# Where the weights are clamped: VectorE's step moved to GpSimd, GpSimd's scaling moved to ScalarE

## The chip, the core and the metric

The kernel runs on one core of one Trainium2 chip. A core has five engines that run side by side [...]: TensorE (PE; its weight loads are shown apart as PEld), VectorE (DVE), ScalarE (ACT), GpSimd (POOL) and SyncE (SP), which here only issues transfers. Each engine works through its own queue in order, so an instruction that waits holds up all that stand behind it. The metric is the time of one execution on the device in microseconds, and the median of several executions is compared. The chip's working memory, SBUF, is read by all engines; TensorE writes its results to PSUM, which GpSimd doesn't read in this kernel.

## The reference, cut to what matters

The program is an attention block and then a gated feed-forward block, all in 32-bit floats.

```python
# q, k, v: (batch 8, heads 8, seq 576, head_dim 64); tau = 0.02
scores = scale * q @ k^T
thresh = max(scores) - tau
scores = where(scores >= thresh, scores, -1e9)
attn   = exp(scores - max(scores));  attn /= sum(attn) + 1e-9
x      = attn @ v          # heads side by side: 4608 tokens x 512
g      = x @ w_gate        # 512 x 1536
out    = (g * sigmoid(g) * (x @ w_val)) @ w_out      # 1536 x 512
```

The three weight matrices come into the program as 64-bit floats. The kernel has to turn them into 32-bit floats itself, piece by piece, and that conversion is what the change is about.

## The kernel before, in words

**Attention of the first batch.** A *pair* is two heads of one batch; there are 32 pairs, four to a batch. In the first batch a slot is one tile of up to 128 queries of one pair against all 576 keys. Eight slots (two tiles of each of the four pairs, `early`) come first, then twelve (the three remaining tiles of each pair, `rest`). In a slot (`scores`) TensorE makes the scores (L407, L413); VectorE takes the row maxima (L424); ScalarE makes the threshold (L427) and the exponentials (L428); VectorE masks and sums (L431, with L433 and L434 for the reciprocal `ri`). The tiles of the early slots are normalized by a scaled identity that ScalarE makes (L447). In the twelve later slots (`t >= TA`) the tile itself is scaled by `ri`: the first head's tile by ScalarE (L441), the second head's by GpSimd (L439). The last tile of each pair, 64 queries, holds both heads in one tile and so needs one scaling only. Then `flip` turns the tile on TensorE (L469, L471, and the ends L474, L476, L480), ScalarE copies it out of PSUM (L477, L481, L483), and `attend_tile` multiplies it with v (L500, L503), which ScalarE copies to `xall` (L505). Into the later slots TensorE is also given the first products with the gate and value weights (L517); ScalarE makes the tanh of the gates (L532, L533), VectorE the product (L541), and GpSimd the last factor (L548, `gates`).

**The weights.** They come in 24 pieces of 768 elements a partition. `fetch_weights` has SyncE load the 64-bit words of a piece into one of several places (L280, L277). `split_weights` and `join_weights` then make 32-bit floats:

- ScalarE takes the upper words (L291) and the lower words (L292), the latter into one of three buffers `los`;
- VectorE clamps the upper part between two constants (L298), shifts it left by three bits (L302), and puts the sign back from the upper word (L305);
- GpSimd adds the lower part (L307), after which the piece is a weight and its place is free again.

A piece is split in one slot and joined in the next. There are three exceptions: one slot joins a piece that it has itself split (at about 62 us in the profile), and two slots join two pieces at once (at about 78 and 100 us; `double` in the code), of which the second was split in the same slot. In the double join both clamps come first, then both shifts, then the rest. In the first batch 21 pieces are joined and 22 are split.

**The order of the work.** For the first batch the order on each engine is the order of the lines, written out by hand. For the other seven batches a planner (class `Plan`) sets it: each step is a job with an engine, a cost and the jobs that it depends on, and for each engine the planner takes the job that can start first, by rank. `rest_of_weights` gives the planner what is left of the conversion: the piece that is split but not joined (`lo` is set), and those not yet split (`lo is None`). Its lines are L820 and L823 (ScalarE), L828, L830 and L832 (VectorE) and L834 (GpSimd). The work of a slot there stands in `slot_rest` (maxima L1673 and L1675, exponentials L1698, masks L1700), and GpSimd and ScalarE share the scaling of the tiles (L1723, L1726).

**GpSimd's queue in the first batch** holds the scaling of q (L340), the adds (L307), the scalings of the second head (L439) and the gate products (L548).

Of the kernel before, what the change touches and what calls it, by code (L numbers as in the profile page):

```python
# [13 lines left out]
AF = mybir.ActivationFunctionType  # L14
ALU = mybir.AluOpType
# [12 lines left out]
class Plan:  # L28
# [12 lines left out]
    def job(self, eng, took, fn, *deps, rank=1, lag=0.0, moves=0.0):  # L41
        j = Job(eng, took, fn, rank, lag, moves)
        for d in deps:
            if isinstance(d, Job) and d.end is None:
                d.then.append(j)
                j.waits += 1
            elif d is not None:
                j.ready = max(j.ready, self.after(d, eng) if isinstance(d, Job) else d + self.HOP)
        if not j.waits:
            self.open[eng].append(j)  # L50
        return j
# [61 lines left out]
def kernel(  # L113
# [11 lines left out]
    nc = tc.nc  # L125
# [157 lines left out]
    def words(place, dst, w):  # L283
        return places[place].bitcast(U32).rearrange("p (m n w) -> p m n w", m=dst.shape[1], w=2)[:, :, :, w]

    def split_weights():
        if fetched:
            dst, place = fetched.popleft()
            lo = los[0].rearrange("p (m n) -> p m n", m=dst.shape[1])
            los.rotate(1)  # L290
            nc.scalar.activation(dst, words(place, dst, 1).bitcast(F32), AF.Abs, scale=2.0 ** -96)  # L291
            nc.scalar.activation(lo, words(place, dst, 0), AF.Identity, bias=minus2, scale=-2.0 ** -51)  # L292
            split.append((dst, place, lo))

    def join_weights(n=1):
        steps = [split.popleft() for _ in range(min(n, len(split)))]
        for up, place, lo in steps:
            nc.vector.tensor_scalar(out=up, in0=up, scalar1=1.875 * 2.0 ** -80, scalar2=2.0 ** -111,  # L298
                                    op0=ALU.min, op1=ALU.max)
        for up, place, lo in steps:  # L300
            ub = up.bitcast(U32)
            nc.vector.tensor_scalar(out=ub, in0=ub, scalar1=3, scalar2=None, op0=ALU.logical_shift_left)  # L302
        for up, place, lo in steps:
            ub = up.bitcast(U32)
            nc.vector.scalar_tensor_tensor(out=ub, in0=words(place, up, 1), scalar=0x80000000, in1=ub,  # L305
                                           op0=ALU.bitwise_and, op1=ALU.bitwise_xor)
            nc.gpsimd.tensor_tensor(out=ub, in0=ub, in1=lo.bitcast(U32), op=ALU.add)  # L307
            joined.append(up)
            used.discard(place)
# [82 lines left out]
    def turned(t):  # L392
        return TA <= t < NT
# [4 lines left out]
    def scores(seg, t):  # L398
        qT, kT = seg["qT"], seg["kT"]
        q0 = t * P - seg["q0"]  # L400
        if t < NT:
            pss = [ps_s.tile([P, 2, 512], F32, name="sc") for _ in range(2)]
            for h, hs in enumerate(heads):
                cut_ = D if turned(t) and h == 1 else 0
                for n, lo, to in [(0, 0, D), (0, D, SH), (1, 0, SH)] if cut_ else [(0, 0, SH), (1, 0, SH)]:
                    at_ = (n * SH + lo - cut_) % S
                    nc.tensor.matmul(pss[h][:, n, lo:to], qT[hs, q0:q0 + P], kT[hs, at_:at_ + to - lo],  # L407
                                     start=True, stop=True)
        else:
            pss = [ps_s.tile([P, 2, 512], F32, name="sc")]  # L410
            for n, h in ((0, 0), (1, 1), (1, 0), (0, 1)):
                hs = heads[h]
                nc.tensor.matmul(pss[0][hs, n, 0:SH], qT[hs, q0:q0 + D], kT[hs, n * SH:(n + 1) * SH],  # L413
                                 start=True, stop=True)
        nm, th, ri, tot = statistics("nm", "th", "ri", "tot")
        sm = sums[0]
        sums.rotate(1)
        m = len(pss)
        scs = [ps[:, :, 0:SH] for ps in pss]
        both = pbufs[0].rearrange("p h s -> p (h s)")[:, KM:KM + P]  # L420
        ps = [pbufs[0][:, x, :].rearrange("p (n s) -> p n s", n=2) for x in range(m)]
        pbufs.rotate(1)
        for x in range(m):
            nc.vector.tensor_reduce(out=nm[:, x:x + 1], in_=scs[x], axis=AX.XY, op=ALU.max, negate=True)  # L424
        yield
        for x in range(m):
            nc.scalar.activation(th[:, x:x + 1], nm[:, x:x + 1], AF.Identity, bias=cut, scale=-1.0)  # L427
            nc.scalar.activation(ps[x], scs[x], AF.Exp, bias=nm[:, x:x + 1])  # L428
        yield
        for x in range(m):  # L430
            nc.vector.scalar_tensor_tensor(out=ps[x], in0=scs[x], scalar=th[:, x:x + 1], in1=ps[x],  # L431
                                           op0=ALU.is_ge, op1=ALU.mult, accum_out=sm[:, x, 0:1])
        nc.vector.tensor_reduce(out=tot[:, 0:m], in_=sm[:, 0:m, 0:3:2], axis=AX.X, op=ALU.add)  # L433
        nc.vector.reciprocal(out=ri[:, 0:m], in_=tot[:, 0:m])  # L434
        units = [ident] * m
        if t >= TA:
            for x in range(m):
                if x % 2:
                    nc.gpsimd.tensor_scalar(out=ps[x], in0=ps[x], scalar1=ri[:, x:x + 1], scalar2=None, op0=ALU.mult)  # L439
                else:  # L440
                    nc.scalar.activation(ps[x], ps[x], AF.Copy, scale=ri[:, x:x + 1])  # L441
        yield
        if t < TA:
            units = [dbufs[0][:, x, :] for x in range(m)]
            dbufs.rotate(1)
            for x in range(m):
                nc.scalar.activation(units[x], ident, AF.Copy, scale=ri[:, x:x + 1])  # L447
        unflipped.append((seg, t, both, [(p.rearrange("p n s -> p (n s)"), unit) for p, unit in zip(ps, units)]))
        yield
# [277 lines left out]
    job, pe = plan.job, plan.pe  # L727
# [72 lines left out]
    def rest_of_weights():  # L800

        todo = [(dst, None, place, lo) for dst, place, lo in split] + [(dst, None, place, None) for dst, place in fetched]
        todo += [(dst, srcs, place, None) for dst, srcs, place in wpieces]
        done, joins = {}, []
        for dst, srcs, place, lo in todo:
            m = dst.shape[1]
            j = None
            if srcs:
                def fetch(dst=dst, srcs=srcs, place=place):
                    to = places[place].bitcast(U64).rearrange("p (m n) -> p m n", m=nf)  # L810
                    nc.sync.dma_start(out=to, in_=srcs[0])

                j = job("SP", 0.1, fetch, done.get(place), lag=5.0)
            if lo is None:
                lo = los[0].rearrange("p (m n) -> p m n", m=m)
                los.rotate(1)
                before = joins[-3] if len(joins) > 2 else None

                def up_part(dst=dst, place=place):
                    nc.scalar.activation(dst, words(place, dst, 1).bitcast(F32), AF.Abs, scale=2.0 ** -96)  # L820

                def lo_part(dst=dst, place=place, lo=lo):
                    nc.scalar.activation(lo, words(place, dst, 0), AF.Identity, bias=minus2, scale=-2.0 ** -51)  # L823

                j = job("ACT", 0.93, up_part, j, done.get(place), rank=2)
                j = job("ACT", 1.03, lo_part, j, before, rank=2)
            ub = dst.bitcast(U32)
            j = job("DVE", 0.6, lambda dst=dst: nc.vector.tensor_scalar(  # L828
                out=dst, in0=dst, scalar1=1.875 * 2.0 ** -80, scalar2=2.0 ** -111, op0=ALU.min, op1=ALU.max), j, rank=2)
            j = job("DVE", 0.6, lambda ub=ub: nc.vector.tensor_scalar(  # L830
                out=ub, in0=ub, scalar1=3, scalar2=None, op0=ALU.logical_shift_left), j, rank=2)
            j = job("DVE", 0.96, lambda ub=ub, dst=dst, place=place: nc.vector.scalar_tensor_tensor(  # L832
                out=ub, in0=words(place, dst, 1), scalar=0x80000000, in1=ub, op0=ALU.bitwise_and, op1=ALU.bitwise_xor), j, rank=2)
            j = job("POOL", 1.85, lambda ub=ub, lo=lo: nc.gpsimd.tensor_tensor(out=ub, in0=ub, in1=lo.bitcast(U32), op=ALU.add), j, rank=2)  # L834
            joins.append(j)
            done[place] = j
        return joins
# [1063 lines left out]
    for s, (n, x) in enumerate((n, x) for n in range(len(halved)) for x in range(NU3)):  # L1901
# [29 lines left out]
        if s in WS:  # L1931
            g, place = WS[s]
# [24 lines left out]
    for c in (B - 1, B):  # L1957
# [4 lines left out]
        if c < B:  # L1962
            w = SM // 2
            j = []
# [43 lines left out]
```

## Time and profile before

| | |
|---|---|
| Median of 3 runs | 1380.48 us (1378.73 to 1381.02) |
| Profiled execution, its own time | 1379.44 us |
| Its span, first to last instruction | 1377.3 us |
| Busy: TensorE, VectorE, ScalarE, GpSimd | 1356.8, 1081.5, 875.1, 700.2 us |
| Same from 0 to 160 us | 147.5, 134.9, 124.6, 76.2 us |
| Clamp L298: 21 times, alone / longest | 0.54 / 2.23 us |
| Shift L302: 21 times, alone / beside L439 | 0.56 / 0.98 us |
| Sign L305: 21 times | 0.96 us |
| Add L307 on GpSimd: 21 times | 1.81 us |
| Scaling L439 on GpSimd, 576 elements: 8 times | 1.94 us |
| Scaling L441 on ScalarE, 576 elements: 12 times | 0.79 us |
| Scaling L340 / L1788 of q on GpSimd: 256, 320, 576 elements | 0.92, 1.08, 1.72 us |

In rows of the profile a duration runs from the start to the end of one instruction; on ScalarE and VectorE the next one starts a little before the end of the last, so 12 scalings of 0.79 us follow each other at some 0.67. The brackets at the end of a row say how long the engine sat idle before it, and what ended that.

### The profile page before, as it was taken

The numbers are of one execution on the slowest core, as the hardware profiler recorded it, in microseconds if no ns is written. First come the engines' busy times: TensorE is split into PE (matmuls) and PEld (weight loads), VectorE is DVE, ScalarE is ACT, GpSimd is POOL, SyncE is SP. The second block draws the span as 40 slices with busy tenths as digits, with TensorE's granted clock in tenths as the row PEclk, the third lists the DMA queues.
The fourth block names the chain that finished last, engine by engine and source line by source line (L and its number), as shares of the span: only waits on it lengthen the run. The fifth ranks groups of instructions, "written<-read, shape, count | busy, mean of one in ns | idle before, by whom it ended". The sixth has DMA issues, their size and how long they took to land.

```text
span 1377.3 us, 39288 instructions
## 1 busy us (share of the span) xinstructions
PE 1356.8 (99%) x15630; PEld 1116.4 (81%) x15630; DVE 1081.5 (79%) x2829; ACT 875.1 (64%) x2278; POOL 700.2 (51%) x649
## 2 busy tenths in 40 slices
PE   9988999999999999999999999999999999999998
PEld 6666787778778778887788888878887888999998
DVE  7988988887887777787678877877777776687786
ACT  6888766676755767767766766776677764330330
POOL 2456498844484669533974378436943593000000
PEclk9999999999999999999999999999999999999999
DMA  8734413465513541555155523553065404423421
GB/s 176 208 105 142 99 36 98 122 188 143 174 48 126 143 115 42 170 143 143 32 153 133 146 56 121 139 143 96 27 186 157 112 19 143 158 80 138 154 69 32
DMA packets 208295, 162.33 MB, mean 118 GB/s; under 512 B 166128, under 2 KB 180464, under 8 KB 202736
## 3 DMA queue, kind: packets, MB, share of 16 engines
q1 hardware_dynamic: 203920, 158.86, 40.9%
q8 instruction: 124, 2.03, 0.6%
q10 hardware_dynamic: 4192, 0.95, 0.3%
q14 instruction: 59, 0.48, 0.1%
HBM read 138.28 MB, written 21.50 MB: 116 GB/s over the span
## 4 chain that ended last, share of the span: by engine, by line
PE 91%; DVE 4%; ACT 2%; SPq 1%; DMA 1%; issue 1%; ACTq 0%; DVEq 0%
PE pb L940 18%; PE pa L940 12%; PE px L1420 12%; PE sc L1652 10%; PE xa L1749 9%; PE pe L940 9%; PE po L1216 5%; PE py L1429 5%; PE sc L1101 2%; PE pg L1147 2%; PE pv L1147 2%; PE pv L517 1%; PE pe L1101 1%; SPq L336 1%; PE xa L500 1%
## 5 line engine op out<-in xcount | busy, mean ns | idle before, releaser
L1700 DVE SCALAR_TENSOR_TENSOR pall<-sc,th,pall 128x288 f32<-128x288 f32 x504 | 243.7, 514 | 63.5 <-ACT pall L1698 49.3
L940 PE MATMUL pb<-xall,big 128*128 128x256 f32 x1152 | 273.5, 380 | 0.0
L1698 ACT ACTIVATE pall<-sc,nm 128x288 f32<-128x288 f32 x504 | 231.6, 497 | 34.6 <-DVE pall L1700 34.3
L940 PEld LDWEIGHTS pb<-xall,big 128*128 128x128 f32 x1152 | 216.4, 190 | 31.0 <-issue 2.2
L1728 DVE STREAM_TRANSPOSE pall<-pall 128x576 f32<-128x576 f32 x252 | 190.0, 765 | 59.3 <-ACT pall L1726 42.6
L1726 ACT ACTIVATE pall<-pall,ri 128x288 f32<-128x288 f32 x408 | 186.6, 527 | 25.0 <-DVE ri L1714 24.3
L795 POOL TENSOR_TENSOR hall<-hall,tmp 128x512 f32<-128x512 f32 x80 | 103.6, 1295 | 159.3 <-DVE hall L993 144.0
L940 PE MATMUL pa<-xall,big 128*128 128x256 f32 x768 | 183.3, 382 | 0.0
L940 PEld LDWEIGHTS pa<-xall,big 128*128 128x128 f32 x768 | 143.1, 190 | 22.0 <-issue 2.9
L1652 PE MATMUL sc<-kT,qT 64*32 64x144 f32 (+1 forms) x5376 | 149.8, 345 | 3.4 <-DVE pall L1700 2.2
L1673 DVE TENSOR_REDUCE mx<-sc 128x2 f32<-128x576 f32 x168 | 124.7, 742 | 27.3 <-PE sc L1652 26.9
L1652 PEld LDWEIGHTS sc<-kT,qT 64*32 64x32 f32 x5376 | 97.9, 106 | 57.5 <-issue 21.6
L940 PE MATMUL pe<-xall,big 128*128 128x256 f32 x576 | 137.3, 381 | 0.0
L1749 PE MATMUL xa<-pall,vall 64*32 64x288 f32 x4032 | 132.2, 404 | 1.0 <-DVE hall L993 0.8
L1723 POOL TENSOR_SCALAR pall<-pall,ri 128x288 f32<-128x288 f32 x96 | 95.7, 1010 | 63.6 <-DVE ri L1714 63.5
L940 PEld LDWEIGHTS pe<-xall,big 128*128 128x128 f32 x576 | 108.4, 190 | 17.0 <-issue 2.7
L1749 PEld LDWEIGHTS xa<-pall,vall 64*32 64x32 f32 x4032 | 76.4, 107 | 50.1 <-issue 7.2
L1708 ACT COPY sums<-sums 32x6 f32<-32x6 f32 x336 | 66.6, 198 | 45.1 <-DVE pall L1700 40.5
L1687 ACT COPY mx<-mx 32x6 f32<-32x6 f32 x196 | 38.1, 194 | 60.8 <-DVE mx L1675 58.9
L992 ACT ACTIVATE vall<-tmp 128x512 f32<-128x512 f32 x96 | 60.1, 629 | 23.9 <-POOL tmp L795 9.6
L1429 PE MATMUL py<-wo,hall 128*128 128x256 f32 x336 | 74.8, 379 | 0.0
L1675 DVE TENSOR_REDUCE mx<-sc 128x1 f32<-128x288 f32 x168 | 74.7, 444 | 0.0
(256 smaller groups left out, 2468.2 us busy)
## 6 DMA issues: line engine op xcount, KB each, us to landing
big<-sums_hbm SPq DMA_DIRECT2D x42, 1024.0 KB, 5.3
big<-sums_hbm SPq DMA_DIRECT2D x48, 768.0 KB, 4.8
vall<-in_v_dram SPq DMA_DIRECT2D x112, 144.0 KB, 3.1
out_dram<-big SPq DMA_DIRECT2D x32, 256.0 KB, 3.5
qT<-in_q_dram SPq DMA_DIRECT2D x112, 72.0 KB, 4.8
kT<-in_k_dram SPq DMA_DIRECT2D x112, 72.0 KB, 3.1
wo<-in_moe_w_gate_dram SPq DMA_DIRECT2D x16, 384.0 KB, 3.8
wo<-in_moe_w_val_dram SPq DMA_DIRECT2D x16, 384.0 KB, 4.5
```

The costliest lines, as they stand in the source:

```text
L795: return lambda: nc.gpsimd.tensor_tensor(out=out, in0=a, in1=b, op=op)
L940: nc.tensor.matmul(ps[:, i], w[:, k_, i * P:(i + 1) * P], x[:, k_, :], start=first and i == k_ == 0, stop=True, skip_group_check=True)
L1420: nc.tensor.matmul(ps, a[:, f, :], ws[n][:, f, :], start=bank_ not in begun, stop=True, skip_group_check=True)
L1429: nc.tensor.matmul(ps(), a[:, f, i * P:(i + 1) * P], operands[o][:, f, :], start=first and f == 0, stop=True, skip_group_check=True)
L1652: nc.tensor.matmul(pss[h][(slice(g * G, (g + 1) * G), *part)], qT[hs, col:col + G], kT[hs, c * SH + keys[0]:c * SH + keys[1]], start=True, ...
L1673: rs.append(job("DVE", 0.72, lambda n=n, tile_=tile_: nc.vector.tensor_reduce(out=mx[:, n:n + 2, 0], in_=tile_[:, :, 0:SH], axis=AX.X, op= ...
L1698: ej = job("ACT", 0.42, lambda x=x, n=n: nc.scalar.activation(ps[x], scs[x], AF.Exp, bias=nm[:, n:n + 1]), ej, *((masks[h, 0], masks[h, 1] ...
L1700: masks[x] = job("DVE", 0.45, lambda x=x, n=n: nc.vector.scalar_tensor_tensor(out=ps[x], in0=scs[x], scalar=th[:, n:n + 1], in1=ps[x], op0 ...
L1723: scaled.append(job("POOL", 1.02, lambda x=x, n=n: nc.gpsimd.tensor_scalar(out=x, in0=x, scalar1=ri[:, n:n + 1], scalar2=None, op0=ALU.mul ...
L1726: scaled.append(job("ACT", 0.46, lambda x=x, n=n: nc.scalar.activation(x, x, AF.Copy, scale=ri[:, n:n + 1]), rj, rank=rank))
L1728: seg["turned"].append(job("DVE", 0.72, lambda both=both: nc.vector.transpose(out=both, in_=both), *scaled, rank=rank))
L1749: nc.tensor.matmul(holds[a].ap()[x * G:(x + 1) * G, 0:SH].rearrange("d (i q) -> d i q", q=G), vr[rs, h, j, ds], p[rs, h, :, j, :], start=( ...
```

## The change

The clamp leaves `join_weights` and goes to the end of `split_weights`, on GpSimd, in place and with the same two constants. In the later slots of the first batch ScalarE scales the tiles of both heads, so L439 is gone. In `rest_of_weights` a piece that was split in the first batch has been clamped there, so its clamp L828 on VectorE is left out; the pieces not yet split keep theirs.

```diff
@@ split_weights
             nc.scalar.activation(dst, words(place, dst, 1).bitcast(F32), AF.Abs, scale=2.0 ** -96)
             nc.scalar.activation(lo, words(place, dst, 0), AF.Identity, bias=minus2, scale=-2.0 ** -51)
+            nc.gpsimd.tensor_scalar(out=dst, in0=dst, scalar1=1.875 * 2.0 ** -80, scalar2=2.0 ** -111, op0=ALU.min, op1=ALU.max)
             split.append((dst, place, lo))
@@ join_weights
         steps = [split.popleft() for _ in range(min(n, len(split)))]
-        for up, place, lo in steps:
-            nc.vector.tensor_scalar(out=up, in0=up, scalar1=1.875 * 2.0 ** -80, scalar2=2.0 ** -111,
-                                    op0=ALU.min, op1=ALU.max)
         for up, place, lo in steps:
             ub = up.bitcast(U32)
             nc.vector.tensor_scalar(out=ub, in0=ub, scalar1=3, scalar2=None, op0=ALU.logical_shift_left)
@@ scores
         if t >= TA:
             for x in range(m):
-                if x % 2:
-                    nc.gpsimd.tensor_scalar(out=ps[x], in0=ps[x], scalar1=ri[:, x:x + 1], scalar2=None, op0=ALU.mult)
-                else:
-                    nc.scalar.activation(ps[x], ps[x], AF.Copy, scale=ri[:, x:x + 1])
+                nc.scalar.activation(ps[x], ps[x], AF.Copy, scale=ri[:, x:x + 1])
@@ rest_of_weights
+            inside = lo is not None
             if lo is None:
                 ...
             ub = dst.bitcast(U32)
-            j = job("DVE", 0.6, lambda dst=dst: nc.vector.tensor_scalar(
+            j = j if inside else job("DVE", 0.6, lambda dst=dst: nc.vector.tensor_scalar(
                 out=dst, in0=dst, scalar1=1.875 * 2.0 ** -80, scalar2=2.0 ** -111, op0=ALU.min, op1=ALU.max), j, rank=2)
```

The order of instructions that follows: on GpSimd a piece's clamp stands ahead of the add of the piece before it. From piece 0 on the queue reads clamp 1, add 0, clamp 2, add 1 and so on, with the q scalings and gate products between; around the exceptions it reads clamp 7, add 6, add 7, clamp 8, clamp 9, add 8, a q scaling, clamp 10, add 9, add 10, clamp 11, gate product, clamp 12, add 11, and likewise clamp 14, add 13, add 14, clamp 15, gate product, clamp 16, add 15. TensorE's order and SyncE's are unchanged. In the planner's part the missing job moves some instructions of VectorE, ScalarE and GpSimd by a few places, within about the first ten slots after the first batch.

## The prediction

> **What bounds the kernel now.** I read the page first: engine shares, then the waits of TensorE, then TensorE, VectorE and GpSimd over the first batch in order of time. Sections 1 and 5 of the page and the windows (columns: length, then busy time of PE, PEld, DVE, ACT and POOL with instruction counts, granted clock, DMA share, GB/s):
>
> ```profile
> PE 1356.8 (99%) x15630; PEld 1116.4 (81%) x15630; DVE 1081.5 (79%) x2829; ACT 875.1 (64%) x2278; POOL 700.2 (51%) x649
> 40.00:60.00 20.00, 18.91 (x157) 14.22 (x157) 18.21 (x41) 19.18 (x43) 8.61 (x6) 1.00 0.90 216
> 60.00:80.00 20.00, 17.72 (x138) 13.19 (x139) 17.16 (x30) 16.85 (x30) 10.90 (x6) 1.00 0.40 121
> 100.00:120.00 20.00, 17.00 (x136) 12.71 (x134) 17.55 (x34) 15.80 (x33) 12.97 (x7) 1.00 0.55 197
> ```
>
> TensorE is busy all but 1377.3 - 1356.8 = 20.5 us. Of these, 160 - 147.5 = 12.5 us lie in the first 160 us, the stretch that the change edits. So a gain ends near 12 us; a loss has no such end. The waits of TensorE from 20 to 150 us (total, times, longest):
>
> ```profile
> PE pv L517 <- ACT big L477: 6.4, 4, 2.3
> PE sc L407 <- DVE pall L431: 2.9, 4, 1.0
> ```
>
> The timeline puts its pauses at 28.59 (0.41), 41.66 (0.81), 69.73 (2.28), 84.54 (1.04), 91.58 (1.70), 105.97 (0.65), 109.69 (0.71), 113.40 (1.64), 132.15 (0.80) and 161.77 (1.58). Most have one root. The copies L477 stand in ScalarE's queue behind the exponentials L428, which wait for the row maxima L424, which stand in VectorE's queue behind the weight join L298, L302, L305. VectorE, late with a join, is what ends last here. The timeline shows why it is late:
>
> ```profile
> 62.53 1.83 POOL L307 TENSOR_TENSOR big<-big,extra 128x768 uint32<-128x768 uint32 x1 [0.57 <-ACT big L291]
> 62.55 2.23 DVE L298 TENSOR_SCALAR big<-big 128x768 f32<-128x768 f32 x1 [0.16 <-ACT big L291]
> 70.62 1.87 POOL L439 TENSOR_SCALAR pall<-pall,ri 128x576 f32<-128x576 f32 x1 [2.31 <-DVE ri L434]
> 70.94 0.98 DVE L302 TENSOR_SCALAR big<-big 128x768 uint32<-128x768 uint32 x1
> 84.91 1.27 POOL L548 TENSOR_TENSOR hall<-hall,tmp 128x512 f32<-128x512 f32 x1
> 85.52 1.08 DVE L298 TENSOR_SCALAR big<-big 128x768 f32<-128x768 f32 x1
> ```
>
> A VectorE tensor-scalar takes 0.54 alone. Behind a GpSimd tensor-tensor it waits until that ends (2.23, 1.08); beside a GpSimd tensor-scalar it takes 0.98.
>
> [...] L832[...] took 1.98 at 152.63 behind an add that began at 151.97, against 0.96 alone. [...] 288 elements take 1.00 (L1723), 576 take 1.72 (L1788), so 2.5 ns an element.
>
> **The change, part by part.** Numbering the pieces 0 to 21 in order of their splits:
>
> - Removed: L298 on VectorE, 21 times, 14.6 us in all with its collisions; one L828 of 0.55 in the slots after. L439 on GpSimd, 8 x 1.94 = 15.5 us, and with it its collisions with L302 (0.98 instead of 0.56, so 0.42 a time).
> - Added to GpSimd: 22 clamps. No two-operation tensor-scalar is in the trace. By the line through L1723 and L1788 it is 1.72 + 192 x 0.0025 = 2.2 us. [...] From above: a second operation as dear as the first, 0.28 + 768 x 0.005 = 4.1. I take 2.3, since L439 beside VectorE took 0.22 more than L1788 of its shape[...].
> - Added to ScalarE: 8 scalings L441 at 0.67 from start to start, 5.4 us. Where ScalarE next waits for maxima (2.28 before 82.61, 1.50 before 89.31) that costs nothing; where it runs without a gap, as from 67.5 to 80.3 and 89.3 to 102.1, all behind it is 0.67 later, the next L291 included.
> - The wait moves. L302 now waits for the clamp, a stage longer: ScalarE's L291, then GpSimd. And the GpSimd queue is in order: a new piece's clamp stands ahead of the old piece's add, which stands ahead of gate products and q scalings. No DMA is issued by a moved step; SP refills a place after L305, so its transfers follow VectorE.
>
> Usually a piece is clamped one slot before its L302, and the clamp is hidden. Five times it is not: piece 7 (split and joined in one slot), 10 and 14 (a double join whose second piece was split in that slot), and 11 and 15 (their clamps stand behind the two late adds of the double join). Walking the queues with trace durations and 2.2 us a clamp gives these leads of the changed kernel (plus is ahead):
>
> 1. To 41.7 us. Three L298 go (0.54 + 0.76 + 0.54 = 1.84); two q scalings now overlap L302 and give back some 0.6: +1.2. To 59 us TensorE's slot falls from 5.73 to about 5.57 (scores 1.28 rather than 1.44) three times: **+1.7**.
> 2. Piece 7. L291 ends at 62.5 - 1.7 = 60.8, clamp to 63.1. GpSimd's add of piece 6 is next and ready[...]. L302 and L305 to 66.4, the transpose L705 0.4, maxima at 66.75 against 66.71: **0**.
> 3. Piece 10. L291 comes 0.67 later (L441), ends 77.55; clamp to 79.8; L302 to 80.4, two L305 to 82.3, L705; maxima at 82.7 against 81.86: **-0.85**.
> 4. Piece 11. Add 9 from 81.45 takes 2.39 as at 80.79, add 10 to 85.65, clamp to 87.85[...]; L302 and L305 to 90.5; maxima at 90.45 against 88.53: **-1.9**.
> 5. Pieces 14 and 15, the same again: maxima at 105.95 against 103.25 and 114.15 against 110.36: **-2.7**, then **-3.8**.
> 6. 114 to 142 us: single joins, clamps hidden. VectorE is 0.54 to 0.96 shorter a slot, ScalarE 0.67 longer in some; TensorE's pause at 132.15 (0.80) fills: **-3.0**.
> 7. From 142 us the masks wait for ScalarE, which waits for TensorE's transposes, so the missing L828 (0.55) is slack. After 160 us TensorE is busy within 8 us of the rest and the lead is carried to the end.
>
> At 2.3 a clamp, five deciding pieces add 5 x 0.1: **-3.5 us**. The profiled execution took 1379.44 (span 1377.3 and 2.1 around it): 1382.9. It lies 1.0 under the median shown, 1380.48, so the median becomes **1384.0**.
>
> **Rivals.** (a) *The clamp is cheap; faster.* All in walk items 2 to 5 hangs on its price, about 5 us of total per 1 us of clamp. The lead is zero at 2.2 - 3.0 / 5 = 1.6 us[...]. [...] Against it: 2.5 ns an element for every one-input row. (b) *The clamp is dear; GpSimd becomes the bound.* At 2.9 the five pieces add 3.0 more, 1387; at 4.1 four clamps, four adds and a gate in each 21.8 us (16.4 + 7.3 + 1.3 = 25) no longer fit: 3 us in each of two such rounds on top of 5 x 1.8, about 1399. For it: two operations instead of one. Against: one-input rows are already above the cost of two-input ones per element (1.72 for 576, 1.81 for 768), so both operations may be in the price. (c) [...] the blocks of 1.8, 1.15 and 1.15 fall away, -3.5 becomes +0.5: no change, 1380. Against it: at 62.53 GpSimd won by 0.02 us, and its next instruction needs no semaphore from another engine. (d) *Everything is in slack:* 1380 too; the pauses listed speak against it.
>
> **How the numbers follow.** Forecast 0.47 (its own range 1381.5 to 1387), (b) 0.21, (c) and (d) together 0.18, (a) 0.14. A measurement of this kernel can tell about 0.2%, 2.8 us, from no change, and the forecast lies just past that: two thirds of it, 0.31, count as slower and 0.16 as the same. Slower 0.31 + 0.21 = 0.52; faster 0.13 of (a) and 0.02 of (c) = 0.15; the same 0.16 + 0.16 + 0.01 = 0.33. The range, 1377.5 to 1391, leaves out about half of (a) and the dearer half of (b).
>
> **What would show it.** Right: no clamp row on VectorE, a GpSimd clamp row of 22 at 2.2 to 2.5; L302's waits on GpSimd in a few large pieces (7, 10, 11, 14, 15) rather than spread; TensorE ahead at 59 us and behind at 115; pauses before L517 near 91 and 113 longer; no change of busy time after 200 us. Wrong: a clamp under 1.6 us or over 2.9, L302 starting at the very end of a clamp with a tensor-tensor queued behind it, or a moved order of the planned slots after 140 us that makes TensorE wait there, which I cost at nothing because TensorE has 7 us of its own work (two groups of L1147) in each such slot.

## The result, and the profile after

The changed kernel takes 1383.65 us in the median of 10 runs (1381.25 to 1384.9), the kernel before 1380.05 us (10 runs beside it, 1378.06 to 1381.35). The ratio is 1.0026, with a 95% interval from 1.0016 to 1.0036: 3.6 us slower, where 3.5 were forecast. The number came out by luck: the clamp costs less than half of what was assumed, the first batch loses next to nothing, and most of the 3.6 us lies after 150 us, in a step that the forecast had costed at nothing.

The profiled execution took 1384.36 us, with a span of 1382.3 us. Its engine shares, and its windows for the same three stretches as before (length, then busy time of PE, PEld, DVE, ACT and POOL, granted clock, DMA share, GB/s):

```profile
PE 1360.3 (98%) x15630; PEld 1118.5 (81%) x15630; DVE 1069.2 (77%) x2807; ACT 879.2 (64%) x2286; POOL 708.6 (51%) x663
40.00:60.00 20.00, 19.52 (x169) 14.89 (x170) 16.68 (x37) 17.82 (x41) 12.01 (x9) 1.00 0.91 222
60.00:80.00 20.00, 17.50 (x120) 12.71 (x119) 13.43 (x24) 17.72 (x30) 11.16 (x9) 0.91 0.36 120
100.00:120.00 20.00, 16.95 (x140) 12.46 (x139) 15.84 (x28) 17.30 (x35) 12.76 (x9) 1.00 0.56 197
```

VectorE has 12.3 us less work and TensorE 3.5 us more, for the same 15630 matmuls: the clock column points to why, since it shows 0.91 from 60 to 80 us where the kernel before had 1.00. From 40 to 60 us TensorE is busier than before (19.52 against 18.91 us): there the change wins, as foretold.

The waits of TensorE from 20 to 150 us, which answer to those of before (6.4 us for L477, 2.9 us for L431):

```profile
PE pv L512 <- ACT big L472: 6.6, 4, 2.5
PE tp L464 <- ACT tmp L528: 1.2, 2, 0.6
PE tp L464 <- ACT pall L436: 0.6, 1, 0.6
...
PE sc L405 <- DVE pall L429: 0.2, 1, 0.2
```

The wait for VectorE's masks fell from 2.9 to 0.2 us. The wait for ScalarE's copies did not fall, and its longest is now 2.5 us. A new one stands beside it: the transposes wait for ScalarE's gate copies (L528), 0.6 us a time, because ScalarE now has the second scaling ahead of these. (The kernel with the scalings alone, below, has the same waits.)

The clamps on GpSimd in the first 145 us, by shape (busy time and mean in ns, then idle time before them):

```profile
L293 POOL TENSOR_SCALAR big<-big 128x768 f32<-128x768 f32 x16 | 16.8, 1047 | 33.9 <-ACT big L291 33.9
L293 POOL TENSOR_SCALAR wo<-wo 128x768 f32<-128x768 f32 x6 | 7.4, 1238 | 13.3 <-ACT wo L291 13.3
```

A clamp takes 1.1 us in the mean, not 2.3. The timeline at 61 and 85 us:

```profile
60.72 0.83 POOL L293 TENSOR_SCALAR big<-big 128x768 f32<-128x768 f32 x1 [3.40 <-ACT big L291]
61.51 1.81 POOL L305 TENSOR_TENSOR big<-big,extra 128x768 uint32<-128x768 uint32 x1
61.58 2.17 DVE L300 TENSOR_SCALAR big<-big 128x768 uint32<-128x768 uint32 x1 [2.10 <-POOL big L293]
84.69 1.27 POOL L543 TENSOR_TENSOR hall<-hall,tmp 128x512 f32<-128x512 f32 x1
84.75 1.63 DVE L300 TENSOR_SCALAR big<-big 128x768 uint32<-128x768 uint32 x1 [0.18 <-POOL big L293]
86.41 1.46 DVE L303 SCALAR_TENSOR_TENSOR big<-wo,big 128x768 uint32<-128x768 uint32 x1
```

Alone a clamp takes 0.83 us. What was foretold for a shift behind a clamp holds to 0.2 us: right behind the clamp GpSimd starts its add (L305) or gate product (L543), and the shift, 0.06 or 0.07 us later, lasts until 0.4 us after that has ended. It takes 2.17 and 1.63 instead of 0.56 us, 1.6 and 1.1 us more, where 1.8 and 1.15 were foretold. This comes on top of the wait for the clamp, which the brackets give apart (2.10 and 0.18 us).

Where the time is lost is seen when TensorE's pauses after 150 us are read in order of time (start, length, engine, line, and in brackets the idle time before it and what ended that). The kernel before has one of over 0.25 us in this stretch, until 289 us:

```profile
161.77 2.13 PE L1652 MATMUL sc<-kT,qT 64*32 64x288 f32 x64 [1.58 <-DVE pall L1700]
```

The changed kernel has three, and the first is followed by scores at a low clock (0.50 from 164 to 166 us; 3.57 instead of 2.13 us for the same 64 matmuls):

```profile
163.50 3.57 PE L1648 MATMUL sc<-kT,qT 64*32 64x288 f32 x64 [2.45 <-DVE pall L1696]
183.61 4.68 PE L1745 MATMUL xa<-pall,vall 64*32 64x288 f32 x140 [0.66 <-ACT mx L1683]
229.45 2.13 PE L1648 MATMUL sc<-kT,qT 64*32 64x288 f32 x64 [1.22 <-DVE pall L1696]
```

(2.45 - 1.58) + 0.66 + 1.22 = 2.75 us are new pauses, and 3.57 - 2.13 = 1.44 us clock.

VectorE's queue ahead of these masks tells what is late. Before:

```profile
156.59 0.76 DVE L1790 STREAM_TRANSPOSE kT<-kT 128x576 f32<-128x576 f32 x1
157.55 0.17 DVE L1691 TENSOR_REDUCE nm<-mx 128x6 f32<-128x12 f32 x1 [0.19 <-ACT mx L1687]
157.63 0.77 DVE L1728 STREAM_TRANSPOSE pall<-pall 128x576 f32<-128x576 f32 x1
158.47 0.52 DVE L1700 SCALAR_TENSOR_TENSOR pall<-sc,th,pall 128x288 f32<-128x288 f32 x1
```

And after:

```profile
157.98 1.41 DVE L1724 STREAM_TRANSPOSE pall<-pall 128x576 f32<-128x576 f32 x2
159.32 0.12 DVE L1687 TENSOR_REDUCE nm<-mx 128x6 f32<-128x12 f32 x1
159.37 0.76 DVE L1789 STREAM_TRANSPOSE qT<-qT 128x576 f32<-128x576 f32 x1
160.20 0.52 DVE L1696 SCALAR_TENSOR_TENSOR pall<-sc,th,pall 128x288 f32<-128x288 f32 x1
```

With one job of 0.6 us less in its books the planner has put two transposes of `pall` ahead of these masks, where there was one, and also the transpose of `qT`, which came behind them before (at 163.25 us). TensorE waits for the masks. They start at 160.20 instead of 158.47 us; of these 1.7 us TensorE was 0.9 late already at 137 us.

### The profile page after: what moved, and what is told of

Same layout as the page of the kernel before. It is cut to its first block, busy times and chain, and to the rows that moved or that the text cites. A ratio compares the mean times of both kernels' runs of the same rounds, so it can differ in the third digit from the quotient of the medians.

```text
span 1382.3 us, 39260 instructions
## 1 busy us (share of the span) xinstructions
PE 1360.3 (98%) x15630; PEld 1118.5 (81%) x15630; DVE 1069.2 (77%) x2807; ACT 879.2 (64%) x2286; POOL 708.6 (51%) x663
## 4 chain that ended last, share of the span: by engine, by line
PE 92%; DVE 4%; ACT 2%; issue 1%; POOL 1%; DMA 1%; SPq 0%; DVEq 0%; ACTq 0%; POOLq 0%
PE pb L936 18%; PE pa L936 12%; PE px L1416 12%; PE sc L1648 10%; PE xa L1745 9%; PE pe L936 9%; PE po L1212 5%; PE py L1425 5%; PE sc L1097 2%; PE pg L1143 2%; PE pe L1097 1%; PE sc L405 1%; PE pv L1143 1%; PE pv L512 1%; PE tp L466 1%; PE xa L495 1%
```

## The experiments

The theories. *The forecast's*: the first batch loses, because the clamp makes joins late; the missing planner's clamp is slack. *The planner's*: the moved order of the planned slots costs the 3.6 us. A third is about TensorE's *clock*: that it falls behind pauses such as those of 2.50 and 2.11 us in the changed kernel's profile (to 0.71 from 66 to 71 us, to 0.70 from 90 to 95), and that this is part of the loss. All runs stand beside runs of the kernel before on the same chip; its median was 1380.18 us in the first four, 1379.93 in the next four, 1379.66 in the next three and 1380.32 in the last.

### The planner's clamp put back

```diff
-            j = j if inside else job("DVE", 0.6, lambda dst=dst: nc.vector.tensor_scalar(
+            j = job("DVE", 0.6, lambda dst=dst: nc.vector.tensor_scalar(
```

> The changed kernel with one part undone: the planner's clamp of the piece split in the first batch stays on VectorE, although GpSimd has clamped it (clamping twice changes nothing), so the planned slots have the order of before. Forecast as recorded (waits for the clamp in the first batch; the missing planner job is slack): no change from the changed kernel, 1383.5. Theory from the two traces (TensorE is 0.87 behind at 151 us, 1.73 at 163.5, 4.8 at 229, so over half is lost in planned slots whose order moved): some 2.5 us faster than the changed kernel, near 1381; lead of TensorE at 140 us unchanged, the pause at 163.5 back to about 1.6, that at 229 gone.

Measured: 1380.02 us, ratio 1.0001 (0.9993 to 1.0009). All that differs from the changed kernel is one VectorE instruction more, and the order that the planner then chooses; the 3.6 us are gone. Its windows from 160 to 260 us:

```profile
160.00:180.00 20.00, 18.36 (x196) 14.72 (x195) 18.39 (x49) 15.46 (x41) 11.12 (x11) 1.00 0.28 62
180.00:220.00 40.00, 39.70 (x652) 32.01 (x651) 33.84 (x101) 27.87 (x81) 39.56 (x37) 1.00 0.19 39
220.00:260.00 40.00, 39.89 (x494) 31.55 (x500) 35.94 (x110) 27.02 (x77) 34.56 (x37) 1.00 0.43 131
```

The changed kernel has 17.55, 39.23 and 38.78 us there.

### The planner's part alone

The kernel before, with GpSimd's clamp for the last piece of the first batch only, and with the planner as in the changed kernel:

```diff
-            j = job("DVE", 0.6, lambda dst=dst: nc.vector.tensor_scalar(
+            j = j if inside else job("DVE", 0.6, lambda dst=dst: nc.vector.tensor_scalar(
```

> The kernel before in the whole first batch, its clamps on VectorE and its scaling shared as it was, except that the last piece of the weights, the one that the planner joins in the second batch, is clamped on GpSimd and the planner's clamp of it (0.55 us of VectorE) is left out, so that the planned slots stand in the order of the changed kernel. The forecast's theory (the loss lies in the first batch and the missing planner's clamp is slack): 1380.2 us, ratio within 0.9990 to 1.0010, and TensorE waits for L1696 as before (1.6 us). The planner theory (the moved order of the planned slots costs the whole 3.6 us): 1383 to 1384.5 us, ratio 1.002 to 1.003, with TensorE's wait for the masks at 160 us near 2.4 us and busy shares of 180 to 260 us as in the changed kernel (39.2 and 38.8 of 40 us).

Measured: 1383.36 us, ratio 1.0027 (1.0016 to 1.0037). TensorE's pauses, which are those of the changed kernel though the first batch is that of before:

```profile
164.40 2.13 PE L1657 MATMUL sc<-kT,qT 64*32 64x288 f32 x64 [2.64 <-DVE pall L1705]
183.04 4.68 PE L1754 MATMUL xa<-pall,vall 64*32 64x288 f32 x140 [0.65 <-ACT mx L1692]
228.88 2.13 PE L1657 MATMUL sc<-kT,qT 64*32 64x288 f32 x64 [1.22 <-DVE pall L1705]
```

The forecast's theory falls. This part alone costs 3.4 us, (2.64 - 1.58) + 0.65 + 1.22 = 2.9 us of it in pauses. Here the clock stayed up after the first pause (1.00 from 160 to 180 us). In this profile it fell once, to 0.91 in the window from 60 to 80 us, behind a pause of 2.27 us before 69.73 us that the kernel before has too (2.28 us, with the clock at 1.00); from there TensorE became 1.6 us late (93.16 instead of 91.58 us at the next value product), and that has nothing to do with the planner.

### The order without the instruction

```diff
-            j = j if inside else job("DVE", 0.6, lambda dst=dst: nc.vector.tensor_scalar(
+            j = job("DVE", 0.6, lambda dst=dst, inside=inside: inside or nc.vector.tensor_scalar(
```

> The changed kernel, with the planner's clamp kept as a job of 0.6 us that issues no instruction: the planned slots stand in the order of the kernel before, and VectorE has still 0.55 us less work. It tells the order from the missing instruction. Order theory: 1380 us, ratio 0.999 to 1.001, 180 to 260 us busy as before (39.7 to 39.9 of 40 us each). Missing instruction theory (something that VectorE now does sooner collides): 1383.6 us, ratio 1.002 to 1.003. The forecast's theory (first batch): 1383.6 us too, but the run with the planner's clamp put back already speaks against it.

Measured: 1381.17 us, ratio 1.0009 (1.0001 to 1.0017). The profile has the pause of before at the masks (1.57 us), none at 183 and 229 us, and busy times of 39.71 and 39.89 us from 180 to 260 us. So it is the order, not the missing 0.55 us, that makes the pauses. The median is 1.1 us over that of the run with the clamp in place; the intervals overlap, and whether anything stands behind it was not settled. In the two profiles it doesn't come from the planned slots: TensorE is 1.1 us behind at 41 us already (41.30 against 40.16 us) and 1.0 at the masks (163.71 against 162.75 us).

### The clamps alone, and the scalings alone

Both are the kernel before with one part of the change, and with the planner as before. The clamps alone:

```diff
             nc.scalar.activation(lo, words(place, dst, 0), AF.Identity, bias=minus2, scale=-2.0 ** -51)
+            nc.gpsimd.tensor_scalar(out=dst, in0=dst, scalar1=1.875 * 2.0 ** -80, scalar2=2.0 ** -111, op0=ALU.min, op1=ALU.max)
...
-            nc.vector.tensor_scalar(out=up, in0=up, scalar1=1.875 * 2.0 ** -80, scalar2=2.0 ** -111,
-                                    op0=ALU.min, op1=ALU.max)
```

> The kernel before with only the clamps of the first batch moved to GpSimd; second-head scaling stays on GpSimd, planner's clamp stays. Forecast as recorded with the clamp at 2.3 us: slower than before by 2 to 4. Theory from the traces (a clamp takes 0.83 alone, 1.05 to 1.4 beside VectorE): the 1.85 us won by 59 us stay to a good part, 0 to 1.5 us faster than before, 1378.5 to 1380.

The scalings alone:

```diff
-                if x % 2:
-                    nc.gpsimd.tensor_scalar(out=ps[x], in0=ps[x], scalar1=ri[:, x:x + 1], scalar2=None, op0=ALU.mult)
-                else:
-                    nc.scalar.activation(ps[x], ps[x], AF.Copy, scale=ri[:, x:x + 1])
+                nc.scalar.activation(ps[x], ps[x], AF.Copy, scale=ri[:, x:x + 1])
```

> The kernel before with only the scaling moved to ScalarE; clamps stay on VectorE, planner unchanged. Forecast as recorded has 0.67 us of lateness in the slots where ScalarE has no gap, and 0.42 us saved on each of 8 shifts: within 1 us of before. Theory from the traces: the two pauses of 0.6 at the transposes appear, and before the L517 of those slots nothing is won: 1 to 1.5 us slower than before, 1381.4.

Measured: clamps alone 1379.62 us, ratio 0.9994 (0.9986 to 1.0002); scalings alone 1381.31 us, ratio 1.0008 (1.0000 to 1.0016). Neither differs from before by as much as the planner's part. With the clamps alone TensorE has two new pauses, in which GpSimd's scaling comes late behind a clamp and a gate product:

```profile
87.98 0.66 PE L467 MATMUL tp<-pall 128*128 128x128 f32 x4 [2.41 <-POOL pall L437]
110.86 1.11 PE L467 MATMUL tp<-pall 128*128 128x128 f32 x4 [2.04 <-POOL pall L437]
```

### The change with the scaling back on GpSimd

```diff
-                nc.scalar.activation(ps[x], ps[x], AF.Copy, scale=ri[:, x:x + 1])
+                if x % 2:
+                    nc.gpsimd.tensor_scalar(out=ps[x], in0=ps[x], scalar1=ri[:, x:x + 1], scalar2=None, op0=ALU.mult)
+                else:
+                    nc.scalar.activation(ps[x], ps[x], AF.Copy, scale=ri[:, x:x + 1])
```

> The changed kernel with the other part undone: the second head's tiles of the later slots are scaled by GpSimd again; clamps stay on GpSimd, the planner's part as changed. Forecast as recorded: GpSimd has 8 x 1.94 us more before its clamps and adds, so the clamps of pieces 7, 10, 11, 14 and 15 come later still: slower than the changed kernel by 2 or more, 1386. Theory from the traces (ScalarE's 8 extra scalings make the pauses before the transposes at 118 and 137, 0.6 each, and hold the maxima's exponentials): faster than the changed kernel by 1 to 2 us in the first batch, 1382; the loss after 150 us stays.

Measured: 1382.63 us, ratio 1.0017 (1.0009 to 1.0025), 1 us under the changed kernel, with 4.4 us of waits for the planned masks (4.3 in the changed kernel, 2.2 before) and 4.8 us for GpSimd's scalings. The planner's part costs here too: it is all that tells this kernel from the one with the clamps alone, which took 3 us less. Both have a mean clock of 0.9969, so these 3 us are not the clock.

### Every clamp twice

In the changed kernel, after GpSimd's clamp:

```diff
+            nc.gpsimd.tensor_scalar(out=dst, in0=dst, scalar1=1.875 * 2.0 ** -80, scalar2=2.0 ** -111, op0=ALU.min, op1=ALU.max)
```

> The changed kernel with every clamp of the first batch done twice on GpSimd (22 more instructions, the second does nothing new): GpSimd has 22 x 0.83 to 1.4 us more work and each join comes later by one clamp. The forecast's sum (a clamp at 2.3 us, joins late by it reach the maxima and TensorE nearly in full): 5 us more per us of clamp, so with 0.9 us more 1388 us, ratio 1.005 to 1.007. Trace theory (VectorE waited only three times, 2.9 us in all, for a clamp, and most joins have slack): 1383.5 to 1385.5, ratio 1.0025 to 1.004.

Measured: 1389.71 us, ratio 1.0069 (1.0053 to 1.0085), 6.1 us over the changed kernel. The second clamp took 0.92 us in the mean. The pauses before the value product in this run, at places where the changed kernel has 2.50 and 1.69 us:

```profile
69.48 2.93 PE L513 MATMUL pv<-xall,big 128*128 128x256 f32 x6 [3.43 <-ACT big L473]
...
118.39 1.57 PE L513 MATMUL pv<-xall,big 128*128 128x256 f32 x6 [2.52 <-ACT big L473]
```

The pause between them is shorter than in the changed kernel (1.69 instead of 2.11 us). VectorE's waits for the clamps (total, times, longest), in the changed kernel and in this one:

```profile
DVE big L300 <- POOL big L293: 2.9, 3, 2.1
DVE big L301 <- POOL big L294: 6.2, 4, 2.9
```

TensorE reaches the third value product at 118.39 instead of 113.55 us, 4.8 us later. Here the forecast's theory holds: its slope, 5 us of time for 1 us of clamp, gives 4.6 for 0.92 us, and 6.1 was measured. The trace theory, with slack behind most joins, falls. A part of the 6.1 us may be clock: the mean clock was 0.9952 against 0.9975, which by the slope in the last section goes with 2 us.

### Filling the pauses

In the changed kernel, and in the one with the planner's clamp back, ahead of the four value products, 5, 4, 3 and 0 times:

```diff
+            nc.tensor.matmul(ends[0][:, P:P + TC], ones[:, 0:P], ones, start=True, stop=True)
```

> The changed kernel with 12 dummy matmuls into unused columns of a bank (5, 4, 3 and 0 of them ahead of the four value products of the first batch, some 0.43 us each), so that TensorE is not idle where it waits for the copies L472 [...]. Clock theory (the pauses over 2 us halve the clock for some 3 us, which cost 1.4 us at 68 us and 1.0 us at 92 us): clock 1.00 in 60:100, TensorE up to 2 us sooner at 142 us, time 1381.5 to 1383. If what is won there is lost again at the masks at 160 us, or if the dummies delay the products by themselves: 1383 to 1385, ratio 1.002 to 1.003.

> The changed kernel with the planner's clamp put back and the same 12 dummy matmuls. Clock theory: 1377.5 to 1379.5 us, ratio 0.998 to 0.9995, faster than both kernels. If the first batch's lead is given back later: 1380 us, ratio 0.9995 to 1.0005.

Measured: 1387.49 us, ratio 1.0055 (1.0043 to 1.0067), and 1383.91 us, ratio 1.0035 (1.0023 to 1.0047). The dummies filled nothing. They waited themselves, for ScalarE's copy out of the bank that they wrote to, up to 3.2 us. A second attempt wrote into the bank of the value product:

```diff
+            nc.tensor.matmul(ps[:, 0], ones[:, 0:P], ones, start=True, stop=True)
```

> The changed kernel with 12 dummy matmuls as before (5, 4, 3 and 0), but into the bank of the value product itself, ahead of the matmuls that overwrite it, so that they wait for no copy of ScalarE; TensorE's pauses of 2.5, 2.1 and 1.7 us ahead of L512 are filled with 2.2, 1.7 and 1.3 us of work. Clock theory (pauses over 2 us halve the granted clock for some 3 us, 1.4 us lost at 68 us and 1.0 us at 92 us): clock 1.00 in 60:100, TensorE 1.5 to 2.5 us sooner at 142 us; with the masks at 160 us unchanged the time is 1381.5 to 1383. If what is won there is lost again at 160 us: 1383.6, ratio 1.002 to 1.003. If the dummies wait too or come late: over 1384.

> The same dummies in the changed kernel with the planner's clamp put back. Clock theory: 1377.5 to 1379.3 us, ratio 0.998 to 0.9995, faster than both kernels. If the lead won in the first batch is given back later: 1380 us, ratio 0.9995 to 1.0005.

Measured: 1386.03 us, ratio 1.0039 (1.0026 to 1.0052), and 1382.37 us, ratio 1.0017 (1.0011 to 1.0024). They waited again, as the changed kernel's row shows when filled (its first ten matmuls are the five dummies, two each):

```profile
68.40 2.43 PE L512 MATMUL pv<-pall 128*128 128x256 f32 x10 [2.51 <-ACT big L473]
```

The other two groups of dummies waited 2.12 and 1.74 us. A dummy reads nothing that ScalarE writes there, so these waits before the value product are for the PSUM bank, which the copies of the transposed tiles have to empty first, and not for data; the wait's name doesn't tell the two apart. What a fallen clock costs these runs don't tell, since no pause was filled. They price delay: from the first of the dummies to the row behind them five take 2.26 us (68.40 to 70.66) and four 1.83 (91.68 to 93.51), so one more is 0.43 us, and 12 are 5.2 us of TensorE's time. The first attempt made both kernels nearly 4 us slower, the second 2.4 us.

### Two scalings on ScalarE, six on GpSimd

The kernel with the clamps alone, and:

```diff
+    scaled_by = deque([1, 1, 0, 1, 0, 1, 1, 1])
...
-                if x % 2:
+                if x % 2 and scaled_by.popleft():
                     nc.gpsimd.tensor_scalar(out=ps[x], in0=ps[x], scalar1=ri[:, x:x + 1], scalar2=None, op0=ALU.mult)
```

> The kernel before, with the clamps of the first batch on GpSimd, the planner as before, and only two of the eight second-head scalings on ScalarE: the third and the fifth, those for which TensorE waited 2.41 us (at 87.98) and 2.04 us (at 110.86) in the run with the clamps alone. The other six stay on GpSimd. If these two waits are the whole loss there: 1375.5 us, ratio 0.9965. Theory of the shifted pause: GpSimd's late scaling only covers a pause that VectorE's maxima make anyway; the two waits go, and TensorE stands ahead of the value product instead, for the bank that ScalarE's copies empty after the maxima: some 2 us at 89 us and 1.5 us at 112 us, so that only 0.5 us a time are won: 1378.5 to 1379.5 us, ratio 0.9985 to 0.9995.

Measured: 1377.82 us, ratio 0.9985 (0.9978 to 0.9992). It is faster than the kernel before and the changed one, 2.5 us under the runs of before beside it. The pauses lie where the theory of the shifted pause put them:

```profile
66.96 1.56 PE L517 MATMUL pv<-xall,big 128*128 128x256 f32 x6 [1.23 <-ACT big L477]
...
89.05 1.56 PE L517 MATMUL pv<-xall,big 128*128 128x256 f32 x6 [2.12 <-ACT big L477]
...
110.37 1.56 PE L517 MATMUL pv<-xall,big 128*128 128x256 f32 x6 [1.78 <-ACT big L477]
...
158.83 2.13 PE L1653 MATMUL sc<-kT,qT 64*32 64x288 f32 x64 [1.60 <-DVE pall L1701]
```

The waits of 2.41 and 2.04 us for GpSimd are gone and 2.12 and 1.78 us for the bank have come. Behind them is VectorE, as before: the maxima of that tile start at 86.01 us here and at 86.26 us with the clamps alone. After each of these three pauses TensorE starts 2.5 to 3.0 us sooner than in the kernel before (66.96 against 69.73, 89.05 against 91.58, 110.37 against 113.40), and at the masks it is 2.9 us ahead. Beside their own runs of before, this kernel is 1.9 us faster than the clamps alone. That may be the clock and nothing else: the mean clock was 0.9994 against 0.9969, and by the slope in the last section that goes with 2.2 us.

## Why the prediction came out right, by wrong steps

The time at which TensorE reaches the same work, in the profiles of five kernels (us; the first four columns are the rows L500 and three times L517 of the kernel before):

| | v product | value 1 | value 2 | value 3 | masks | last mask pause |
|---|---|---|---|---|---|---|
| before | 59.92 | 69.73 | 91.58 | 113.40 | 161.77 | 289.44 |
| changed | 58.07 | 68.10 | 90.84 | 113.55 | 163.50 | 294.22 |
| planner's clamp back | 58.08 | 68.14 | 90.89 | 113.60 | 162.75 | 290.42 |
| planner's part alone | 59.93 | 69.73 | 93.16 | 114.98 | 164.40 | 293.67 |
| two scalings | 58.20 | 66.96 | 89.05 | 110.37 | 158.83 | 286.49 |

**Step 1, to 59 us, +1.7: right.** Measured 59.92 - 58.07 = +1.85.

**The price of the clamp, 2.3 us: wrong by a factor of two and more.** It takes 0.83 us alone and 1.1 in the mean. This was the condition that the prediction named for its own failure (under 1.6 us), and rival (a) is the one that had the clamp cheap. The 768 elements in 0.83 us are 1.1 ns an element, against a slope of 2.5 ns in the rows of scaling (1.00 us for 288 elements, 1.72 for 576). Those multiply by an operand that holds one number per partition; the clamp has two constants. They were the nearest rows, but not the same operation. Which of the differences makes the price was not tested.

**Steps 2 to 5, leads of 0, -0.85, -1.9, -2.7 and -3.8 at pieces 7, 10, 11, 14 and 15: wrong in size, right in kind.** The order of the queues and the five pieces came as described. So did the shift that lasts until GpSimd's next instruction has ended (2.17 us behind the clamp of piece 7, 1.63 at 84.75 us), and so rival (c), without these blocks, falls. But each of these clamps is 1.4 us shorter than the 2.2 of the walk: the maxima start at 65.08, 80.83, 87.80, 103.11 and 110.50 us, which is +1.63, +1.03, +0.73, +0.14 and -0.14. Doubling the clamp bore out the slope of these steps upwards (4.6 foretold, 6.1 measured); the value put into it was wrong.

**Step 6, -3.0 at 142 us: wrong in size.** At 132 us the lead is 132.15 - 132.39 = -0.24. The pause filled there from 0.80 to 0.31 us, as said; the added scaling on ScalarE, which the step let pass at these slots, makes two pauses of 0.6 us ahead of the transposes, and the lead is -0.9 when the planned slots begin.

**Step 7, the planned slots, 0: this is the step that failed.** It reasoned that a missing VectorE step is slack where TensorE has work. It didn't ask what the planner does when one of its jobs is gone. From value 3 to the last mask pause the kernel before takes 289.44 - 113.40 = 176.0 us, the planner's part alone 178.7, the changed kernel 180.7 and the changed kernel with the planner's clamp back 176.8. The prediction had named such a moved order as what would make it wrong, and had dismissed it because of 7 us of TensorE's own work in each slot; the pauses of 2.45, 0.66 and 1.22 us show that this doesn't cover it.

**How the sum still came out: by two errors of opposite sign, which is luck.** The clamps of the five deciding pieces (at 60.72, 76.94, 83.90, 99.65 and 106.60 us) took 0.82 or 0.83 us. With 0.83 the prediction's own slope gives 3.5 - 5 x (2.3 - 0.83) = -3.9 us, a gain. The planner's part adds 3.4 measured: -0.5. Some 4 us are left to the measured 3.6, and they belong to the first batch: the change without the planner's part came out 0.2 us faster than the runs beside it, not 3.9.

Where that gain went is shown in part. One place is GpSimd's queue. With the clamps alone its scaling stands between the clamp of piece 7 and the add:

```profile
61.07 0.83 POOL L293 TENSOR_SCALAR big<-big 128x768 f32<-128x768 f32 x1 [3.41 <-ACT big L291]
61.88 2.12 POOL L437 TENSOR_SCALAR pall<-pall,ri 128x576 f32<-128x576 f32 x1
61.93 0.56 DVE L300 TENSOR_SCALAR big<-big 128x768 uint32<-128x768 uint32 x1 [2.11 <-POOL big L293]
63.97 1.82 POOL L305 TENSOR_TENSOR big<-big,extra 128x768 uint32<-128x768 uint32 x1
```

VectorE's shift takes 0.56 us there; the maxima start at 64.18 us, and the first value product at 67.19 us after a pause of 1.25 us. With the planner's clamp put back, which differs only in the scalings, the add stands right behind the clamp and the shift takes 2.17 us; the maxima start at 65.11 us, the product at 68.14 us after 2.52 us. So moving the scaling away let the add forward, and the add holds VectorE up.

Another place is the clock: behind the pauses at the first two value products it is 0.71 from 66 to 71 us and 0.70 from 90 to 95 in the changed kernel, and 1.00 in the kernel before. TensorE's order is the same in both kernels, so the same rows can be compared, first changed, then before:

```profile
68.10 2.93 PE L512 MATMUL pv<-xall,big 128*128 128x256 f32 x6 [2.50 <-ACT big L472]
72.33 1.09 PE L495 MATMUL xa<-big,vall 128*64 128x128 f32 x16
69.73 1.56 PE L517 MATMUL pv<-xall,big 128*128 128x256 f32 x6 [2.28 <-ACT big L477]
72.34 1.09 PE L500 MATMUL xa<-big,vall 128*64 128x128 f32 x16
```

With no pause between, TensorE's lead falls from 1.63 to 0.01 us; from 90.84 to 96.06 us it falls again, from 0.74 to -0.85. But the profile of before has a mean clock of 1.000, as only 32 of 114 runs of that kernel have, so these two profiles show more of this than the medians do (0.9985 with the planner's clamp back, 0.9988 before).

At an equal mean clock of 0.999 the kernel before took 1379.96 us in the mean (37 runs), the planner's clamp back 1380.06 (7 runs), two scalings 1378.59 (8 runs) and the clamps alone 1377.46 (3 runs). So what the clamps alone gave back went with a lower clock, and what eight scalings on ScalarE gave back did not. The groups are small and were not made by an experiment; how much belongs to the add, to the scalings' 0.67 us apiece and to the clock stays open.

**The rivals.** (a), the cheap clamp, is what was measured (0.83 us), but the gain that it foretold is not, since it too had nothing for the planner. (b) is excluded by the clamp's duration. (d), all in slack, is excluded by the doubled clamp.

## What to carry to other kernels

Where a planner or scheduler orders part of a kernel, an instruction taken out of its list is two changes: the instruction, and a new order of everything after it. Build both orders and compare them on each engine before costing the removed work at its own length; here 0.55 us less work cost 3.4 us, and a placeholder that keeps the order gave most of it back. When a step is moved to a free engine, move only the instances that are late where they are: with the clamps, two scalings moved won 2.5 us, where eight moved won nothing. And ask what an instruction that goes away was holding apart: here the scaling had stood between the clamp and an add that holds up VectorE (a shift of 2.17 us beside it, and of 0.56 with the scaling between).

## What the runs showed of the hardware that was not expected

**The clock fell behind some pauses of 1.85 to 2.50 us, and not behind others of the same length.** In windows of 5 us the changed kernel's granted clock is 0.71 from 66 to 71 us, 0.70 from 90 to 95 and 0.87 from 160 to 165, each with or behind a pause of 2.50, 2.11 or 2.45 us. While it is down it is halved: it is 0.50 from 69 to 71 us, from 92 to 95 and from 164 to 166, and six matmuls that take 1.56 us took 2.93 at 68 us. With the scalings alone six matmuls took 2.46 us behind a pause of 1.85 us (0.91 from 60 to 80 us). It doesn't happen each time: the kernel before had a pause of 2.28 us in its profile and kept 1.00, the planner's part alone had one of 2.27 at the same place and fell to 0.91 from 60 to 80 us, with 2.12 us for the six matmuls, and the two-scalings kernel had one of 2.12 and kept 1.00. What decides was not found.

Over the 114 runs of the kernel before that stand beside the experiments, those with a mean clock of 1.000 took 1378.90 us in the mean (32 runs), those with 0.997 took 1381.55 (8 runs), so 0.001 of clock goes with some 0.9 us. The mean clock was 0.9988 before, 0.9975 with the change, 0.9979 with the planner's part alone, 0.9969 with the clamps alone and 0.9994 with two scalings. By this slope about 1.2 of the change's 3.6 us, 0.8 of the 3.4 us of the planner's part, and 0.5 of the 2.5 us that two scalings win, go with the clock; that is a correlation over runs, and the experiments meant to test it tested something else.

**GpSimd's price per element is not the same for two operations with one input tensor.** A clamp by two constants over 768 elements took 0.83 us (1.1 ns an element), a scaling by a number per partition over 576 elements took 1.72 us (3.0 ns), both alone.
